# A Nyström attention and two mixture layers on one core: loads of 128 partitions, another grouping of heads, G split straight from its banks, x copies on GpSimd, both squares on ScalarE

## The chip, the core and the metric

The kernel runs on one core of one Trainium2 chip. The core has a matrix engine (PE; its weight loads are shown apart as PEld), VectorE (DVE), ScalarE (ACT), GpSimd (POOL) and SyncE (SP), which here issues nearly all DMAs. The metric is the device time of one execution in microseconds (us).

## The reference

Attention with 32 landmarks over 8 batches, 8 heads, 576 tokens and 64 columns a head; its output x (4608 × 512) goes through a layer with a squared relu, then through one of eight experts for each token.

```python
q_lm = q.reshape(B, H, m, S // m, D).mean(axis=3)     # k_lm alike, m = 32
A, Bm, C = sm(q, k_lm), sm(q_lm, k_lm), sm(q_lm, k)   # scaled softmax of a @ b.T
Z = Bm.T / (norm_1(Bm) * norm_inf(Bm) + 1e-06)
for _ in range(6):
    Z = 2 * Z - Z @ Bm @ Z
x = heads_side_by_side(A @ Z @ C @ v)
x = square(maximum(x @ w_in, 0)) @ w_out              # 512 -> 2048 -> 512
e_idx = argmax(x @ w_gate)                            # one expert for each token
out = gate_w * eom * (maximum(x @ w1[e_idx], 0) @ w2[e_idx])
```

## The kernel before

**Order of the products.** For each batch and head the kernel forms the 32 × 64 matrix wz = Z·C·v, then G = wz·w_in, and only then the product with A: hp = G·Aᵀ is the hidden layer itself. Each operand of a large product is split into two float32r parts, a rounded one and the rest, and three products of parts stand for one (`gb`, `ab`, `wo` hold such pairs).

**The main loop.** `gemm(b, c, f)` goes over 8 batches b, two halves c of 288 tokens and 16 blocks f of 128 hidden rows. For each f PE writes hp (six matmuls) into the pool `hps`, which has one PSUM bank, so the six of f+1 can't begin before ACT has read hp of f. ACT makes r = relu(hp) and gh, its square rounded to float32r; DVE makes g2 = r·r in full and gl = g2 − gh. Two f later (`pend`) `second` runs twelve matmuls of wo with gh and gl into four accumulator banks.

**The side work.** While `gemm` runs batch b, the attention unit of batch b+1 goes along in small steps (`point`, paced by RATES): `sums` of 18 rows for the landmarks (on POOL from batch 2 on), `flipped` (turns a group of four heads of q or k by 32 × 32 transposes on DVE, L480 and L484; two heads then lie on the wrong partitions, so two copies of 32 × 576 on ACT, L491, carry others over, and two transposes of 32 partitions, which overwrite what the copies read, follow them; the two groups of a k or q go together, so four copies come at one place, two places a batch), scores, softmax, `inverse`, `values`. `transposed` does the work of `flipped` on PE for the first two batches. Near the end of a batch `next_g` makes the four G of the next one: eight matmuls into a pair of banks (`two`), an ACT copy gs of each bank (L995), a few steps later an ACT cast gb and two POOL subtracts (`halves`) for the second part.

**The beginning.** `prologue` computes the first batch's unit with nothing to lie beside. Meanwhile `convert` fetches w_in and w_out, which lie in DRAM as 8-byte floats, in pieces of 128 × 512 (`raw`, 524 kB each, four buffers); ACT and POOL make floats of them (`m`, `r`, then `wf` or `w`). Four wf make one G of the first batch, and `first_g` makes two G before the main loop; each wf is also written to DRAM (`win`) for the later batches. Loads of q, k (four DMAs of 32 partitions for a group of four heads), v (three DMAs of 32 partitions), raws and the win writes stand in one queue, SP's.

**Order.** A scheduler sets each engine's order from priorities (URGENT for r, g2, gh, gl and all of the prologue); on each engine instructions then run strictly in that order. After the loop `experts` runs the expert layer, which the change does not touch.

Of the kernel before, what the change touches and what calls it, by code (L numbers as in the profile page):

```python
# [44 lines left out]
CONV = 0.45  # L45
CONV_FIRST = 2
# [24 lines left out]
def head_of(g, j):  # L71

    return j // 2, 2 * g + j % 2
# [18 lines left out]
class Kernel:  # L92
    def __init__(self, tc, ins, out):
# [6 lines left out]
        self.gt, self.at, self.made, self.g_done, self.last_gb, self.last_lo = {}, {}, {}, 0, None, None  # L100
        self.wf, self.wo, self.qk, self.vt, self.wts, self.wis = {}, {}, {}, {}, {}, {}


    def after(self, n, fn):

        self.later.append((self.now + n, fn))

# [115 lines left out]
    def convert_in(self):  # L223

        def job(i):
            n, kp = divmod(i, KD)

            def place():
# [6 lines left out]
                lambda w: self.nc.sync.dma_start(out=self.win_d[n][:, kp], in_=w),  # L235
# [22 lines left out]
    def run(self):  # L258
        tc = self.tc
        with ExitStack() as ctx:  # L260
# [31 lines left out]
            def swap():  # L292
                tmp.close()
                self.wi, self.gs = T("wi", 2), T("gs", 2)
                out_pools(T)
                self.loads = iter([(b, n) for b in range(1, B) for n in range(4)])
                for _ in range(2):
                    self.load_w()
# [109 lines left out]
    def load_next(self, pool=None):  # L408
# [6 lines left out]
        src = (self.k if nm == "k" else self.q)[b, 4 * hg:4 * hg + 4].rearrange("(a g) (l s) d -> g a l (s d)", g=2, s=SEG)  # L415
        for g in range(2):
            for a in range(2):
                p = 64 * g + LM * a
                self.nc.sync.dma_start(out=t[p:p + LM].rearrange("p s d -> p (s d)"), in_=src[g, a])

    def load_v(self, b, g, pool=None):
        if b < B:
            t = self.vt[b, g] = (pool or self.ld).tile([PT, 4, R6 * D], F32, tag="v", name="v", bufs=1)
            src = self.v[b].rearrange("(j g) (l i r) d -> g i l j (r d)", g=2, i=3, r=R6)[g]
            for i in range(3):
                self.nc.sync.dma_start(out=t[LM * i:LM * i + LM], in_=src[i])

    def sums(self, u, nm, hg):
# [4 lines left out]
        if not u["pe"]:  # L433
# [20 lines left out]
    def transposed(self, u, nm, hg, i):  # L454
# [14 lines left out]
        if i == 2 and not (u["b"] == 0 and nm == "q" and hg == 1):  # L469
            self.load_next()  # L470

    def flipped(self, u, nm, hg):
# [17 lines left out]
        for h in (0, 2):  # L490
            self.nc.scalar.copy(out=x[LM * h + LM:LM * h + 2 * LM, 0], in_=x[LM * h:LM * h + LM, 1])  # L491
# [73 lines left out]
    def scores_c(self, u, i):  # L565
# [5 lines left out]
        for g, c, sc in self.products(u, "k", "ql", i):  # L571
            to, src = u["ec"][:, g], sc
            if u["pe"]:
                to = to.rearrange("p (r c i l) -> p c i r l", c=2, i=3, l=LM)[:, c]
                src = src.rearrange("p (i r l) -> p i r l", i=3, l=LM)
            else:
                to = to[:, c * HC:(c + 1) * HC]
# [85 lines left out]
    def values(self, u, hg):  # L663
# [3 lines left out]
        with self.run_of():  # L667
            for r in reversed(range(R6)):
                for h in reversed(range(4)):
# [3 lines left out]
                        rhs=self.vt[b, hg][:, h, r * D:(r + 1) * D],  # L673
# [8 lines left out]
        elif hg == 1:  # L682
            self.load_v(b + 1, 0)

    def inverse(self, u, i):
# [13 lines left out]
        if i == 6:  # L699
            u["wz"] = sm.tile([128, 2, D], F32, tag="wz", name="wz")  # L700
            nc.vector.tensor_tensor(out=u["wz"], in0=was[:, :, LM:], in1=pp[:, :, LM:], op=ALU.add)
# [15 lines left out]
        nc.scalar.copy(out=eu[:, :, 0:LM], in_=pp[:, :, 0:LM])  # L717
        nc.vector.tensor_tensor(out=eu[:, :, LM:], in0=was[:, :, LM:], in1=pp[:, :, LM:], op=ALU.add)

# [56 lines left out]
    def last_values(self, u):  # L776
# [3 lines left out]
        u["wz"] = self.sm.tile([128, 2, D], F32, tag="wz", name="wz")  # L780
        self.nc.vector.tensor_copy(out=u["wz"], in_=w)
# [127 lines left out]
    def prologue(self, right):  # L909
# [15 lines left out]
        while True:  # L925
# [5 lines left out]
            due += CONV  # L931
# [6 lines left out]
    def first_g(self):  # L938

        self.banks = [self.acc]  # L940
        with self.tc.high_priority(URGENT):
# [3 lines left out]
            self.drain()  # L945
        self.banks = [self.aux]

    def chunk(self, b, n, rows):
# [6 lines left out]
        with self.run_of():  # L955
            for g in range(2):
                for j in range(4):
                    p = slice(64 * g, 64 * g + 64)
                    self.matmul(
                        banks[g][32 * j:32 * j + 32], lhsT=self.wts[b][p, 32 * j:32 * j + 32], rhs=rows(j)[p],  # L960
# [5 lines left out]
    def first_g_of(self, n):  # L966
# [5 lines left out]
        t = self.gt[0, n]  # L972
        for g in range(2):
            gb = nc.scalar.copy(out=t[:, 0, g], in_=banks[g])
            lo = nc.vector.tensor_tensor(out=t[:, 1, g], in0=banks[g], in1=t[:, 0, g].bitcast(F32), op=ALU.subtract)
            if n < G_FIRST:
                self.last_gb, self.last_lo = gb, lo
# [8 lines left out]
    def next_g(self, b, n):  # L986
# [5 lines left out]
        t = self.gt[b, n]  # L992
        for g in range(2):
            raw = self.gs.tile([128, 512], F32, tag="gs", name="gs")
            self.nc.scalar.copy(out=raw, in_=banks[g])  # L995
# [550 lines left out]
```

## Time and profile before

| what | value |
|---|---|
| three runs | 1317.33, 1319.91, 1320.98 us (median 1319.91) |
| profiled execution | 1318.15 us, span 1316.3 us |
| PE busy | 1223.3 us, 93% of the span |
| DVE, ACT, POOL busy | 692.7, 590.3, 480.2 us |
| mean granted clock of PE | 0.977 |

The span runs from the first to the last instruction on the engines, and the profiled execution's own time stands 1.9 us above it. The first G begins at 59.57 us; the loop's first batch ends shortly before 200 us, batches 1 to 5 go to about 717 us, batches 6 and 7 to 893 us, and the experts take the rest. A row of a view gives start and length of an instruction, its engine, line and operation, output and input tiles, shape, and in brackets how long the engine had waited and for what.

### The profile page before, as it was taken

The numbers are of one execution on the slowest core, as the hardware profiler recorded it, in microseconds if no ns is written. First come the engines' busy times: TensorE is split into PE (matmuls) and PEld (weight loads), VectorE is DVE, ScalarE is ACT, GpSimd is POOL, SyncE is SP. The second block draws the span as 40 slices with busy tenths as digits, with TensorE's granted clock in tenths as the row PEclk, the third lists the DMA queues.
The fourth block names the chain that finished last, engine by engine and source line by source line (L and its number), as shares of the span: only waits on it lengthen the run. The fifth ranks groups of instructions, "written<-read, shape, count | busy, mean of one in ns | idle before, by whom it ended". The sixth has DMA issues, their size and how long they took to land.

```text
span 1316.3 us, 25740 instructions
## 1 busy us (share of the span) xinstructions
PE 1223.3 (93%) x9834; PEld 1086.7 (83%) x9834; DVE 692.7 (53%) x1641; ACT 590.3 (45%) x1316; POOL 480.2 (36%) x627
## 2 busy tenths in 40 slices
PE   3578899899999999999999999999999999999996
PEld 2367887878888988888888989998888988888885
DVE  5487765865765864864864745453333323233231
ACT  4556464464464464464355354343333424334231
POOL 3776724424432415415313221033333424324220
PEclk9689999999999999999999999999999999999998
DMA  9965324233133124123114220025344445353331
GB/s 255 335 187 153 118 95 119 62 101 120 55 101 119 54 72 146 40 88 132 37 51 151 67 83 19 20 56 147 103 120 142 125 122 147 96 157 88 110 92 38
DMA packets 90205, 142.29 MB, mean 108 GB/s; under 512 B 8222, under 2 KB 63550, under 8 KB 86494
## 3 DMA queue, kind: packets, MB, share of 16 engines
q1 hardware_dynamic: 89646, 139.98, 35.4%
q8 instruction: 79, 1.29, 0.4%
q0 software_dynamic: 288, 0.43, 0.1%
q14 instruction: 48, 0.39, 0.1%
q10 hardware_dynamic: 144, 0.20, 0.0%
HBM read 117.47 MB, written 23.11 MB: 107 GB/s over the span
## 4 chain that ended last, share of the span: by engine, by line
PE 76%; DVE 7%; DMA 5%; ACT 4%; POOL 3%; issue 2%; SPq 1%; DVEq 0%; POOLq 0%; ACTq 0%
PE hp L393 28%; PE acc L393 25%; PE y L393 16%; PE two L389 2%; DMA t<-in_q_dram 2%; PE bank L389 2%; DVE x L480 2%; DMA raw<-in_moe_w_in_dram 2%; PE bank L401 1%; DVE gl L1059 1%; POOL st L436 1%; ACT x L491 1%; DVE x L484 1%; POOL gb L221 1%; DMA v<-in_v_dram 1%
## 5 line engine op out<-in xcount | busy, mean ns | idle before, releaser
L393 PE MATMUL acc<-gh,wo 128*128 128x288 f32 x2048 | 450.9, 299 | 7.0 <-DVE wo L215 6.5
L393 PEld LDWEIGHTS acc<-gh,wo 128*128 128x128 f32 x2048 | 342.0, 190 | 19.2 <-DVE wo L215 8.1
L393 PE MATMUL acc<-gl,wo 128*128 128x288 f32 x1024 | 294.1, 301 | 2.4 <-DVE gl L1059 2.4
L393 PE MATMUL hp<-ab,gb 128*128 128x288 f32 x1536 | 262.9, 307 | 31.4 <-ACT r L1056 29.9
L393 PEld LDWEIGHTS hp<-ab,gb 128*128 128x128 f32 x1536 | 217.8, 191 | 59.1 <-ACT r L1056 39.8
L1057 DVE TENSOR_TENSOR g<-r 128x288 f32<-128x288 f32 x256 | 140.8, 551 | 194.2 <-ACT r L1056 192.3
L393 PE MATMUL y<-s,h 128*128 128x512 f32 (+1 forms) x896 | 223.0, 396 | 0.8 <-ACT h L1291 0.5
L393 PEld LDWEIGHTS hp<-xs,s 128*128 128x128 f32 x1536 | 212.3, 188 | 7.4 <-DVE ls L1502 0.3
L393 PE MATMUL hp<-xs,s 128*128 128x288 f32 x1536 | 217.4, 295 | 0.2 <-DVE ls L1502 0.2
L393 PEld LDWEIGHTS acc<-gl,wo 128*128 128x128 f32 x1024 | 195.4, 191 | 13.5 <-DVE gl L1059 5.8
L1056 ACT ACTIVATE r<-hp 128x288 f32<-128x288 f32 x256 | 105.3, 411 | 207.2 <-PE hp L393 190.4
L393 PEld LDWEIGHTS y<-s,h 128*128 128x128 f32 (+1 forms) x896 | 160.7, 184 | 37.8 <-ACT h L1291 0.7
L221 POOL TENSOR_TENSOR s<-r,s 128x256 fp32r<-128x256 f32 x128 | 102.1, 819 | 235.5 <-ACT s L209 235.5
L1059 DVE TENSOR_TENSOR gl<-g,gh 128x288 fp32r<-128x288 f32 x256 | 144.3, 564 | 37.0 <-ACT gh L1058 19.9
L1294 DVE SCALAR_TENSOR_TENSOR h<-hp,h 128x64 fp32r<-128x64 f32 (+2 forms) x192 | 62.4, 354 | 166.3 <-ACT h L1291 165.9
L221 POOL TENSOR_TENSOR gb<-gs,gb 128x256 fp32r<-128x256 f32 x112 | 90.4, 837 | 135.9 <-ACT gb L1000 135.9
L1291 ACT ACTIVATE h<-hp 128x288 fp32r<-128x288 f32 x128 | 52.5, 412 | 187.8 <-PE hp L393 172.3
L1058 ACT ACTIVATE gh<-r 128x288 fp32r<-128x288 f32 x256 | 114.1, 446 | 39.3 <-PE acc L393 26.2
L209 ACT CAST s<-r 128x512 fp32r<-128x512 f32 x128 | 77.6, 617 | 69.9 <-PE y L393 56.0
L215 DVE TENSOR_TENSOR s<-r,s 128x512 fp32r<-128x512 f32 x64 | 50.2, 784 | 101.6 <-ACT s L209 101.6
L436 POOL TENSOR_TENSOR st<-t 128x288 f32<-128x288 f32 x48 | 42.1, 897 | 96.7 <-DMA t<-in_q_dram 92.0
L221 POOL TENSOR_TENSOR aa<-aa,ma 128x288 f32<-128x288 f32 x60 | 44.2, 760 | 80.2 <-DVE ma L551 60.2
(201 smaller groups left out, 1128.1 us busy)
## 6 DMA issues: line engine op xcount, KB each, us to landing
r<-in_moe_w_dram SPq DMA_DIRECT2D x128, 256.0 KB
wi<-win SPq DMA_DIRECT2D x28, 1024.0 KB
t<-in_k_dram SPq DMA_DIRECT2D x64, 144.0 KB
t<-in_q_dram SPq DMA_DIRECT2D x64, 144.0 KB
v<-in_v_dram SPq DMA_DIRECT2D x48, 192.0 KB
x_d<-x SPq DMA_DIRECT2D x16, 576.0 KB
xr<-x_d SPq DMA_DIRECT2D x16, 576.0 KB
raw<-in_moe_w_in_dram SPq DMA_DIRECT2D x16, 511.8 KB
```

What stands on the lines that cost most here:

```text
L209: hi = self.nc.scalar.copy(out=t[:, 0], in_=raw)
L215: lo_eng.tensor_tensor(out=t[:, 1], in0=raw, in1=t[:, 0].bitcast(F32), op=ALU.subtract)
L221: self.nc.gpsimd.tensor_tensor(out=out[:, p], in0=in0[:, p], in1=in1[:, p], op=op)
L389: self.in_run(lambda: self.nc.tensor.matmul(out, **kw))
L393: mm = self.nc.tensor.matmul(out, **kw)
L436: add = lambda out, in0, in1: self.nc.gpsimd.tensor_tensor(out=out, in0=in0, in1=in1, op=ALU.add)
L1056: nc.scalar.activation(out=r, in_=hp[:, 0:HC], func=ACTF.Relu)
L1057: nc.vector.tensor_tensor(out=g2, in0=r, in1=r, op=ALU.mult)
L1058: nc.scalar.activation(out=gh, in_=r, func=ACTF.Square)
L1059: nc.vector.tensor_tensor(out=gl, in0=g2, in1=gh.bitcast(F32), op=ALU.subtract)
L1291: nc.scalar.activation(out=h[:, t0:t1], in_=hp[:, 0:HC], func=ACTF.Relu)
L1294: nc.vector.scalar_tensor_tensor(out=h[:, to + a:to + z], in0=hp[:, a - t0:z - t0], scalar=0.0, in1=h[:, a:z].bitcast(F32), op0=ALU.max, o ...
```

## The change

A group of four heads of q or k is now loaded by one DMA over 128 partitions, in the natural order of heads, and v by two DMAs of 96 partitions. Which head stands where follows: `head_of`, the operands of `chunk` and `values` and the layout of the scores change, and wz is put together with its halves crossed on every second group of 32 partitions (four DVE instructions in place of one). G of the later batches is split as that of the first was: ACT casts from the bank, DVE subtracts from the bank; gs and the POOL halves go. The four copies in `flipped` move from ACT to POOL, g2 from DVE to ACT, the copy eu in `inverse` from ACT to DVE, and the sums of one early q group from DVE to POOL. `hold` keeps win writes, the loads of the second batch's q, k and v back until the first G in program order, and the first eight wf are converted at a rate of 0.8 a step.

```diff
 def head_of(g, j):
 
-    return j // 2, 2 * g + j % 2
+    return j // 2, 3 - j % 2 if g else j % 2
...
+    def hold(self, fn):
+
+        if self.held is None:
+            fn()
+        else:
+            self.held.append(fn)
...
-                lambda w: self.nc.sync.dma_start(out=self.win_d[n][:, kp], in_=w),
+                lambda w: self.hold(lambda: self.nc.sync.dma_start(out=self.win_d[n][:, kp], in_=w)),
...
-        src = (self.k if nm == "k" else self.q)[b, 4 * hg:4 * hg + 4].rearrange("(a g) (l s) d -> g a l (s d)", g=2, s=SEG)
-        for g in range(2):
-            for a in range(2):
-                p = 64 * g + LM * a
-                self.nc.sync.dma_start(out=t[p:p + LM].rearrange("p s d -> p (s d)"), in_=src[g, a])
+        src = (self.k if nm == "k" else self.q)[b, 4 * hg:4 * hg + 4]
+        self.nc.sync.dma_start(
+            out=t.rearrange("p s d -> p (s d)"), in_=src.rearrange("h (l s) d -> (h l) (s d)", s=SEG)
+        )
...
-            src = self.v[b].rearrange("(j g) (l i r) d -> g i l j (r d)", g=2, i=3, r=R6)[g]
-            for i in range(3):
-                self.nc.sync.dma_start(out=t[LM * i:LM * i + LM], in_=src[i])
+            src = self.v[b].rearrange("(a g i) (p r) d -> a g p i (r d)", g=2, i=2, r=R6)
+            for a in range(2):
+                self.nc.sync.dma_start(out=t[:, 2 * a:2 * a + 2], in_=src[a, g])
...
-        if not u["pe"]:
+        if not u["pe"] or u["early"] and nm == "q" and hg == 1:
...
-            self.load_next()
+            self.hold(self.load_next)
...
         for h in (0, 2):
-            self.nc.scalar.copy(out=x[LM * h + LM:LM * h + 2 * LM, 0], in_=x[LM * h:LM * h + LM, 1])
+            self.nc.gpsimd.tensor_copy(out=x[LM * h + LM:LM * h + 2 * LM, 0], in_=x[LM * h:LM * h + LM, 1])
...
-            self.load_v(b + 1, 0)
+            self.hold(lambda: self.load_v(b + 1, 0))
...
+            for j in range(4):
+                p = slice(32 * j, 32 * j + 32)
+                nc.vector.tensor_tensor(
+                    out=self.crossed(wz, j), in0=was[p, :, LM:], in1=pp[p, :, LM:], op=ALU.add
+                )
...
-        nc.scalar.copy(out=eu[:, :, 0:LM], in_=pp[:, :, 0:LM])
+        nc.vector.tensor_copy(out=eu[:, :, 0:LM], in_=pp[:, :, 0:LM])
...
+    def crossed(self, wz, j):
+
+        t = wz[32 * j:32 * j + 32]
+        return t[:, ::-1] if j % 2 else t
...
-            due += CONV
+            due += CONV if len(self.wf) >= G_FIRST * KD else CONV_SOON
...
+        held, self.held = self.held, None
+        for fn in held:
+            fn()
         self.banks = [self.aux]
...
-        t = self.gt[b, n]
-        for g in range(2):
-            raw = self.gs.tile([128, 512], F32, tag="gs", name="gs")
-            self.nc.scalar.copy(out=raw, in_=banks[g])
-            self.after(2 + g, lambda g=g, raw=raw: self.split_g(t, g, raw))
-
-    def split_g(self, t, g, raw):
-
-        self.nc.scalar.copy(out=t[:, 0, g], in_=raw)
-        self.halves(t[:, 1, g], raw, t[:, 0, g].bitcast(F32), ALU.subtract)
+        self.split_g(self.gt[b, n], banks)
+
+    def split_g(self, t, banks):
+
+        nc = self.nc
+        for g in range(2):
+            gb = nc.scalar.copy(out=t[:, 0, g], in_=banks[g])
+            lo = nc.vector.tensor_tensor(out=t[:, 1, g], in0=banks[g], in1=t[:, 0, g].bitcast(F32), op=ALU.subtract)
+        return gb, lo
...
                     nc.scalar.activation(out=r, in_=hp[:, 0:HC], func=ACTF.Relu)
-                    nc.vector.tensor_tensor(out=g2, in0=r, in1=r, op=ALU.mult)
                     nc.scalar.activation(out=gh, in_=r, func=ACTF.Square)
+                    nc.scalar.activation(out=g2, in_=r, func=ACTF.Square)
                     nc.vector.tensor_tensor(out=gl, in0=g2, in1=gh.bitcast(F32), op=ALU.subtract)
```

**SP, from its first instruction on.** t is a group of q or k, raw a piece of w_in, win the copy of w_in in DRAM. Before:

```order
L419 DMA t<-in_k_dram 32x1152 x8
L419 DMA t<-in_q_dram 32x1152 x3
L419 DMA t<-in_k_dram 32x1152 x4
L419 DMA t<-in_q_dram 32x1152
L419 DMA t<-in_k_dram 32x1152 x4
L419 DMA t<-in_q_dram 32x1152 x4
L161 DMA raw<-in_moe_w_in_dram 128x2047 x3
L426 DMA v<-in_v_dram 32x4x384 x6
L161 DMA raw<-in_moe_w_in_dram 128x2047 x2
L235 DMA win_124<-wf 128x512
L161 DMA raw<-in_moe_w_in_dram 128x2047 x2
L235 DMA win_124<-wf 128x512 x2
```

And now:

```order
L425 DMA t<-in_k_dram 128x1152 x2
L425 DMA t<-in_q_dram 128x1152 x2
L170 DMA raw<-in_moe_w_in_dram 128x2047 x3
L434 DMA v<-in_v_dram 96x2x384 x4
L170 DMA raw<-in_moe_w_in_dram 128x2047
L425 DMA t<-in_k_dram 128x1152 x2
L170 DMA raw<-in_moe_w_in_dram 128x2047
L244 DMA win_112<-wf 128x512
L170 DMA raw<-in_moe_w_in_dram 128x2047 x2
L244 DMA win_112<-wf 128x512 x2
L170 DMA raw<-in_moe_w_in_dram 128x2047
L244 DMA win_112<-wf 128x512
```

A group of heads is one row's DMA instead of four, the first q stands behind two k instead of behind eight loads, and the k of the second batch (the third and fifth rows before, the pair behind the fourth raw now) has moved behind four raws.

**ACT, in batch 2's first half, beside the flip of a later batch's k.** r, gh and g are the relu and the squares, x the copies, aa an exponential, eu a copy of the inverse. Before:

```order
L1056 ACTIVATE r<-hp 128x288
L1058 ACTIVATE gh<-r 128x288
L491 COPY x<-x 32x576 x2
L1056 ACTIVATE r<-hp 128x288
L491 COPY x<-x 32x576 x2
L1058 ACTIVATE gh<-r 128x288
L1056 ACTIVATE r<-hp 128x288
L557 ACTIVATE aa<-aa 128x576
L717 COPY eu<-bank 128x2x32
L1058 ACTIVATE gh<-r 128x288
L557 ACTIVATE aa<-aa 128x576
L1056 ACTIVATE r<-hp 128x288
```

And now, at the same place:

```order
L1076 ACTIVATE r<-hp 128x288
L1077 ACTIVATE gh<-r 128x288
L1078 ACTIVATE g_4227<-r 128x288
L1076 ACTIVATE r<-hp 128x288
L1077 ACTIVATE gh<-r 128x288
L1078 ACTIVATE g_4262<-r 128x288
L565 ACTIVATE aa<-aa 128x576
L1076 ACTIVATE r<-hp 128x288
L1077 ACTIVATE gh<-r 128x288
L1078 ACTIVATE g_4301<-r 128x288
L565 ACTIVATE aa<-aa 128x576
L1076 ACTIVATE r<-hp 128x288
```

The four copies and eu are gone from between r and gh, and one more square, g, stands behind each gh.

**POOL, at the same flip.** gb is the split of G, ab and aa parts of the attention matrix, st and sums the landmark sums. Before:

```order
L436 TENSOR_TENSOR sums<-st 128x128
L221 TENSOR_TENSOR gb<-gs,gb 128x256 x4
L221 TENSOR_TENSOR ab<-at,ab 128x288 x2
L221 TENSOR_TENSOR aa<-aa,ma 128x288 x4
L436 TENSOR_TENSOR st<-t 128x288 x2
L436 TENSOR_TENSOR st<-st 128x256
L436 TENSOR_TENSOR st<-st 128x128
L221 TENSOR_TENSOR aa<-aa,ma 128x288 x2
```

And now:

```order
L444 TENSOR_TENSOR sums<-st 128x128
L499 COPY x<-x 32x576 x2
L230 TENSOR_TENSOR ab<-at,ab 128x288 x2
L499 COPY x<-x 32x576 x2
L230 TENSOR_TENSOR aa<-aa,ma 128x288 x4
L444 TENSOR_TENSOR st<-t 128x288 x2
L230 TENSOR_TENSOR aa<-aa,ma 128x288 x2
```

The four gb halves are gone; two of the four copies stand ahead of ab, two behind it.

## Rows read from the trace of the kernel before

**Rows 1.** Busy time in three stretches; the columns stand in the first row.

```profile
core 0: us, PE busy (x) PEld busy (x) DVE busy (x) ACT busy (x) POOL busy (x), PEclk, DMA share, GB/s
59.60:200.00 140.40, 122.44 (x1062) 102.69 (x1063) 106.10 (x207) 83.90 (x193) 84.16 (x114) 0.94 0.50 152
200.00:717.00 517.00, 487.21 (x4502) 434.65 (x4501) 334.86 (x814) 254.57 (x606) 189.42 (x262) 0.99 0.29 89
717.00:893.00 176.00, 175.54 (x1411) 166.21 (x1411) 93.86 (x233) 76.56 (x179) 39.11 (x49) 1.00 0.19 58
```

**Rows 2.** ACT, then PE, in order of time, up to the first G.

```profile
49.31 0.77 ACT L173 ACTIVATE m<-raw 128x512 f16<-128x512 bf16 x1 [1.99 <-DMA raw<-in_moe_w_in_dram]
...
59.57 1.11 PE L389 MATMUL bank<-wf,wt 64*32 64x512 f32 x8
```

**Rows 3.** Waits of PE, 200 to 717: total us, times, longest.

```profile
PE hp L393 <- ACT r L1056: 25.0, 23, 2.6
PE two L389 <- ACT gs L995: 1.6, 3, 0.9
```

**Rows 4.** PE in order of time: four of its 23 waits for r.

```profile
209.73 1.06 PE L393 MATMUL hp<-ab,gb 128*128 128x288 f32 x6 [2.58 <-ACT r L1056]
...
237.89 1.06 PE L393 MATMUL hp<-ab,gb 128*128 128x288 f32 x6 [1.09 <-ACT r L1056]
...
508.27 1.05 PE L393 MATMUL hp<-ab,gb 128*128 128x288 f32 x6 [1.48 <-ACT r L1056]
...
688.96 1.07 PE L393 MATMUL hp<-ab,gb 128*128 128x288 f32 x6 [1.40 <-ACT r L1056]
```

**Rows 5.** ACT in order of time, shortly ahead of the first two of these.

```profile
206.73 0.59 ACT L995 COPY gs<-two 128x512 f32<-128x512 f32 x1 [4.42 <-POOL gb L221]
...
235.71 1.37 ACT L491 COPY x<-x 32x576 f32<-32x576 f32 x2
```

**Rows 6.** Waits of ACT and of POOL, 200 to 717.

```profile
ACT gs L995 <- POOL gb L221: 24.2, 14, 4.4
...
POOL ab L221 <- ACT ab L209: 72.6, 7, 22.1
```

**Rows 7.** Groups, 200 to 717: count, busy us, mean ns, idle before.

```profile
L1057 DVE TENSOR_TENSOR g<-r 128x288 f32<-128x288 f32 x156 | 85.7, 550 | 117.1 <-ACT r L1056 115.9
...
L1058 ACT ACTIVATE gh<-r 128x288 fp32r<-128x288 f32 x157 | 69.9, 446 | 25.9 <-PE acc L393 15.0 <-DVE g L1057 3.9 <-DVE ma L559 3.7
...
L1059 DVE TENSOR_TENSOR gl<-g,gh 128x288 fp32r<-128x288 f32 x157 | 88.7, 565 | 23.2 <-ACT gh L1058 13.5 <-PE bank L401 0.9
...
L491 ACT COPY x<-x 32x576 f32<-32x576 f32 x40 | 26.8, 671 | 4.5 <-DVE x L480 3.3
...
L221 POOL TENSOR_TENSOR gb<-gs,gb 128x256 fp32r<-128x256 f32 x88 | 70.8, 833 | 84.0 <-ACT gb L1000 83.9
```

**Rows 8.** Groups of POOL, whole span, columns as in rows 7.

```profile
L452 POOL COPY sums<-sums 128x64 f32<-128x64 f32 x8 | 1.9, 240 | 22.6 <-DVE sums L447 22.6
...
L175 POOL CAST m<-raw 128x512 f16<-128x512 bf16 x24 | 19.0, 805 | 3.6 <-DMA raw<-in_moe_w_in_dram 3.6
...
L221 POOL TENSOR_TENSOR wf<-m,r 128x256 int32<-128x256 int32 x32 | 23.4, 760 | 8.0 <-ACT r L176 7.7
```

**Rows 9.** Waits of PE, 59.6 to 200.

```profile
PE acc L393 <- DVE wo L215: 6.5, 5, 3.0
PE hp L393 <- ACT r L1056: 5.0, 6, 1.5
```

**Rows 10.** DMA rate in stretches of the beginning, columns as in rows 1.

```profile
8.00:18.00 10.00, 3.32 (x12) 2.36 (x12) 4.33 (x4) 1.93 (x5) 0.51 (x3) 1.00 1.04 230
22.00:28.00 6.00, 3.19 (x51) 1.35 (x52) 2.29 (x8) 4.53 (x14) 4.82 (x7) 1.00 1.10 230
28.00:34.00 6.00, 4.86 (x52) 3.23 (x50) 4.37 (x20) 4.33 (x10) 3.11 (x5) 1.00 1.02 393
```

**Rows 11.** DVE in order of time, while POOL splits a G.

```profile
211.08 1.07 DVE L1059 TENSOR_TENSOR gl<-g,gh 128x288 fp32r<-128x288 f32 x1 [0.48 <-ACT gh L1058]
```

More of the change, by code (lines that the diff above doesn't have):

```diff
@@ L45 @@
 CONV = 0.45
+CONV_SOON = 0.8
 CONV_FIRST = 2
@@ L100, in __init__ @@
         self.gt, self.at, self.made, self.g_done, self.last_gb, self.last_lo = {}, {}, {}, 0, None, None
+        self.held = []
         self.wf, self.wo, self.qk, self.vt, self.wts, self.wis = {}, {}, {}, {}, {}, {}
@@ L293, in swap @@
                 tmp.close()
-                self.wi, self.gs = T("wi", 2), T("gs", 2)
+                self.wi = T("wi", 2)
                 out_pools(T)
@@ L573, in scores_c @@
             if u["pe"]:
-                to = to.rearrange("p (r c i l) -> p c i r l", c=2, i=3, l=LM)[:, c]
+                to = to.rearrange("p (r c l i) -> p c i r l", c=2, i=3, l=LM)[:, c]
                 src = src.rearrange("p (i r l) -> p i r l", i=3, l=LM)
             else:
-                to = to[:, c * HC:(c + 1) * HC]
+                to = to.rearrange("p (r l i) -> p r i l", i=3, l=LM)[:, 3 * c:3 * c + 3]
+                src = src.rearrange("p (r i l) -> p r i l", i=3, l=LM)
             nc.scalar.copy(out=to, in_=src)
@@ L672, in values @@
                         lhsT=u["et"][:, R6 * hg + r, 32 * h:32 * h + 32],
-                        rhs=self.vt[b, hg][:, h, r * D:(r + 1) * D],
+                        rhs=self.vt[b, hg][:, h ^ hg, r * D:(r + 1) * D],
                         start=(r == R6 - 1), stop=(r == 0),
@@ L699, in inverse @@
         if i == 6:
-            u["wz"] = sm.tile([128, 2, D], F32, tag="wz", name="wz")
-            nc.vector.tensor_tensor(out=u["wz"], in0=was[:, :, LM:], in1=pp[:, :, LM:], op=ALU.add)
+            wz = u["wz"] = sm.tile([128, 2, D], F32, tag="wz", name="wz")
+            for j in range(4):
[3 more added lines that the diff above has]
+                )
             return
@@ L779, in last_values @@
         self.blocks(w, u["ef"], u["w0"])
-        u["wz"] = self.sm.tile([128, 2, D], F32, tag="wz", name="wz")
-        self.nc.vector.tensor_copy(out=u["wz"], in_=w)
+        wz = u["wz"] = self.sm.tile([128, 2, D], F32, tag="wz", name="wz")
+        for j in range(4):
+            self.nc.vector.tensor_copy(out=self.crossed(wz, j), in_=w[32 * j:32 * j + 32])
     def diagonal(self, u, x):
@@ L957, in chunk @@
                 for j in range(4):
-                    p = slice(64 * g, 64 * g + 64)
+                    half = g ^ (j % 2)
+                    p = slice(64 * half, 64 * half + 64)
                     self.matmul(
-                        banks[g][32 * j:32 * j + 32], lhsT=self.wts[b][p, 32 * j:32 * j + 32], rhs=rows(j)[p],
+                        banks[g][32 * j:32 * j + 32], lhsT=self.wts[b][p, 32 * j:32 * j + 32],
+                        rhs=rows(2 * (j // 2) + g)[p],
                         start=True, stop=True,
@@ L971, in first_g_of @@
         banks = self.chunk(0, n, lambda j: self.wf[n * KD + j])
-        t = self.gt[0, n]
-        for g in range(2):
[L974 to L977, printed above, removed]
+        gb, lo = self.split_g(self.gt[0, n], banks)
+        if n < G_FIRST:
+            self.last_gb, self.last_lo = gb, lo
     def load_w(self):
```

## The prediction

> **What bounds the kernel now.** I read the busy time by stretches first, since one change rarely acts on the whole span. From 717 to 893 us PE is busy 175.54 of 176.00 us [rows 1], so nothing can be won there, and the experts behind it are not touched. From 200 to 717 us PE is busy 487.21 of 517.00, which leaves 29.8 us of idle time; from 59.6 to 200 it is 122.44 of 140.40, which leaves 18.0. Ahead of 59.6 PE has not begun its large products: the eight matmuls of the first G stand at 59.57, and on ACT a conversion at 49.31 still waited 1.99 us for a piece of w_in by DMA [rows 2]. So there are three places: the loads of the beginning, the first batch, and the five batches after it.
>
> In the five batches the chain of waits is short. PE waited 25.0 us in 23 waits for r, before the first product of a new hp, and 1.6 us for gs [rows 3]. Looked up in order of time, 21 of the 23 (20.9 us) fall at ten places where ACT makes the four x copies, two in each batch: the first is the 1.09 us at 237.89 and the last the 1.40 at 688.96; the other two, 2.58 at 209.73 and 1.48 at 508.27, 4.1 us together, are not at such a place [rows 4]. What ACT did just ahead shows why. At 235.71 it ran two x copies in a row, 1.37 us, while r and the squares stood behind them; at 206.73 a gs copy had waited 4.42 us for a gb subtract of POOL to free its buffer [rows 5], one of 14 such waits of 24.2 us in all [rows 6]. On average DVE is busy 334.86 and ACT 254.57 of 517 us [rows 1]; it is their order at a dozen places that costs.
>
> **The change part by part.**
>
> *Five batches, 200 to 717 us.* 157 f in 517 us are 3.3 us each. ACT loses the 40 copies of 671 ns, 26.8 us, and takes a square of 446 ns (the row of gh, which is the same operation on the same shape) for each f, 70 us [rows 7]. It also loses 40 gs copies of 0.59 us (five batches, four G, two banks), 24 us. Its busy time goes from 255 to about 275 of 517: no bound. DVE loses 85.7 us of g2 and takes 40 subtracts of 512 columns, each at most 1.0 us (565 ns of gl, for 288 columns, scaled). POOL loses 70.8 us of gb and takes 40 copies.
> At a place with copies ACT loses 4 × 0.671 = 2.7 us and gains the three squares that stand there among its twelve rows, 1.3 us. Net 1.35 us against a wait of 20.9 / 10 = 2.1 us: if the squares count in full, 13.5 us come back at the ten places; if they fit into ACT's idle time between two r, all 20.9. I take 16, nearer the lower end, because ACT is late exactly there.
> The waits for gs (1.6) and for r behind gs (4.1) lose their cause, since nothing on ACT waits for POOL's subtract any more; in its place the pair of banks comes free only after DVE's second subtract. Nothing gained to 5.7; I take 5, since the next G follows two or three f later.
> The square delays the next r elsewhere only where ACT is late for another reason. The 20 G are such places, with two casts; at most 20 × 0.446 = 8.9 us, at least 0; I take 3, because r is not ready before hp is, and PE's waits for r lie only at the places named.
> Sum: −16 − 5 + 3 = −18, bounds −26.6 and −4.6. The copies of eu, 64 columns, which ACT loses and DVE takes, and the three more small adds for wz are counted at nothing: they lie beside PE's matmuls and help ACT where they hurt DVE; if DVE were the late one, they would cost about what the copy of 64 columns on POOL shows, 240 ns [rows 8], five or six times a batch.
>
> *First batch, 59.6 to 200 us.* Here DVE is the late engine: PE waited 6.5 us for the split of wo on DVE and 5.0 for r [rows 9]. Sixteen g2 of the first half leave DVE, 8.8 us of 550 ns, and 7.1 us of squares come to ACT, which was busy 83.90 of 140.40 [rows 1]. I take −3; bounds −9 (most of both waits) and +7 (all squares late).
>
> *The beginning.* SP's order is what decides, so I counted it up to the eleventh raw, the one that ACT waited for. Before and now the same bytes stand ahead of it: 28 loads of 32 × 1152 floats or their equal (4.13 MB), 1.18 MB of v, eleven raws, five win writes. So the hold itself moves nothing on this queue, and what is left is the rate. With loads of 32 partitions the queues moved 230 GB/s from 8 to 18 us, with those of v 230 from 22 to 28, and with raws of 128 partitions 393 from 28 to 34, all with the DMA engines fully busy [rows 10]. At 393 the q and k take 10.5 us instead of 18.0: −7.4. v on 96 partitions lies between 230 and 393, so 0 to −2.1; I take −1. ACT now converts 15 pieces instead of 14 ahead of the first wt; a piece takes one pass r and every second time a pass m on ACT, 0.77 us a pass [rows 2], so +1.2. Together −7, bounds −9.5 and 0.
> The Trainium skill, "SBUF — State Buffer", section "Door 1: The DMA port swizzle", says that a transfer of 32 partitions reaches half of the sixteen ports into SBUF; the trace agrees, 230 against 393 GB/s. By its table 96 partitions reach all ports, but half of these carry twice the rows: an estimate of 12/16 of 393, 295 GB/s, by which v would save 1.1 us and the sum would stay.
>
> *All.* −18 − 3 − 7 = −28. The profiled execution took 1318.15 us, so 1290 us for one like it; the median of the runs is 1.76 above it, so **1292 us**. By the bounds of the parts the same case goes from 1275 to 1322.
>
> **Rivals.**
>
> *The loads don't bring the first G forward (1299 us).* Between the wait at 49.31 and the first G at 59.57 lie 10 us without one for DMA [rows 2]. If raws come 7 us sooner, the conversion must keep up: POOL gives each raw two halves of 760 ns and every second one a cast of 805 ns [rows 8], 1.9 us, and gets eight adds of an early q besides (at most 6 us by the same 760); ACT and the scores share the rest. Then part or all of the 7 us is lost. For it: the halves of wf waited 7.7 us for ACT's r [rows 8], so ACT holds the conversion up too; against it: the row at 49.31 waits for DMA, behind ten pieces. 1290 + 7 + 1.8 = 1299.
>
> *The squares are paid for (1307 us).* ACT carries the chain hp, r, gh, and an r that is late by one square holds PE. If it is late in 34 of the 157 f, seven a batch around G and softmax, that is 34 × 0.446 = 15 us of the 18 lost again: 1290 + 15 + 1.8 = 1307. For it: ACT was late at the ten places; against it: a mean idle time of half of ACT.
>
> *Slower (1336 us): the copies wait on POOL.* Of the twelve places six now have two copies ahead of ab on POOL and two behind it, as the order shows. POOL's ab waited 72.6 us in 7 waits for ACT, 10.4 each [rows 6]; the second pair stands behind that. The transposes of 32 partitions on DVE wait for the copies, and the gl of four following f stand among them. A copy of 32 × 576 is not in the trace on POOL. Its bounds are 240 ns (64 columns) and 805 (a cast of 512 columns) [rows 8]; along the line through both 576 columns cost 0.9 us. So the last copy comes 10.4 + 4 × 0.9 = 14 us late, gl has two f of slack, 6.6 us, and 7.4 us are lost at each of six places, +44. It outweighs the gain from 28 / 6 = 4.7 us a place, copies about 11 us late. Against it: ab's two parts were waited for since POOL had nothing else ready; the scheduler has put the copies there with ab's cast near in ACT's order, and all of ab's waits need not fall at flips.
> While POOL subtracted a G, a gl of DVE took 1.07 us [rows 11] against a mean of 565 ns [rows 7]: the two engines hold each other up. The Trainium skill, "SBUF — State Buffer", section "Who interferes with whom", says that a DVE instruction with two inputs in SBUF and a GpSimd instruction that reads SBUF exclude each other for a whole instruction; the row agrees in direction. By that rule each copy could start up to 0.57 us later, four of them 2.3, and this rival would be reached sooner by that; in return 157 g2 with two inputs leave DVE.
>
> **How the numbers follow.** The sum as worked out 0.60, the loads in vain 0.20, the squares paid for 0.11, the copies late 0.06, something else 0.03. The forecast is the first case's 1292 us. For 8 in 10 the range goes from 1276, a little above that case's lower bound, to 1314, which takes in the first two rivals and leaves out the third: 0.06 of it, 0.03 of the rest and some 0.08 of the tails lie outside. A difference of 0.3%, 4 us, is about what a measurement of this kernel can tell from no change. Faster than 1316: nearly all of the first three cases, 0.89; between 1316 and 1324: their tails, 0.04; above: the third rival and part of the rest, 0.07.
>
> **What would show it.** The DMA rate up to 20 us near 393 instead of 230, and the first G at about 52 us; if the rate is there and the G still at 59, the first rival holds. PE's waits for r from 200 to 717 at under 10 us instead of 25.0, none after an x copy, and none for gs; if they stand at other places behind a square, the second. POOL's x copies at about 0.9 us, and DVE's transposes of 32 partitions waiting for them: if more than 5 us at a place, with PE waiting for gl, the third. Stretches after batch 6 and the experts as long as before. The prediction is wrong above all if the order of the engines, which is fixed beforehand from estimated durations, puts an instruction ahead of r or gl that comes late on the chip: no row of the kernel before can show that.

## The result, and the profile after

The changed kernel takes **1259.53 us** (median of four runs, 1259.2 to 1260.13), against 1320.45 us for the kernel before on the same chip: a ratio of 0.9543, 95% interval 0.9527 to 0.9560. 61 us were gained where 28 were forecast, and the time lies below the range. Three single runs further on, one of a_x (1373.1 us), one of u_gs4 (2344.5) and one of the kernel before (1968.1), stood far above the others of their kernel, and the medians are without them.

To see where they went I read from ACT's rows in order of time when r was made for the 32nd and for the 192nd f: these mark the ends of the first batch and of batch 5, in either kernel.

| us | before | after | change | forecast |
|---|---|---|---|---|
| first G begins | 59.57 | 50.71 | −8.9 | −7 |
| first G to 32nd r | 125.3 | 119.2 | −6.1 | −3 |
| 32nd to 192nd r (batches 1 to 5) | 528.7 | 486.6 | −42.1 | −18 |
| 192nd r to the end of the span | 602.8 | 601.0 | −1.8 | 0 |

So the miss lies in batches 1 to 5. The first three rows below, of the changed kernel, answer to [rows 1], with its columns; the fourth is its batches 1 to 5, 169.91 to 656.49 us:

```profile
59.60:200.00 140.40, 129.83 (x1186) 113.31 (x1187) 89.44 (x186) 89.55 (x219) 79.89 (x112) 0.97 0.43 149
200.00:717.00 517.00, 515.86 (x4816) 467.81 (x4816) 305.05 (x828) 278.24 (x706) 145.89 (x219) 1.00 0.28 93
717.00:893.00 176.00, 175.55 (x1259) 163.13 (x1259) 56.78 (x150) 86.06 (x200) 39.45 (x38) 1.00 0.23 69
...
169.91:656.49 486.58, 485.44 (x4596) 436.57 (x4595) 294.09 (x775) 266.10 (x676) 148.25 (x224) 1.00 0.29 99
```

And the same five batches of the kernel before, with a piece of them around one flip:

```profile
184.88:713.54 528.66, 496.79 (x4586) 441.88 (x4585) 347.51 (x852) 263.55 (x627) 187.70 (x260) 0.99 0.29 89
...
430.90:433.90 3.00, 1.26 (x8) 0.83 (x6) 2.88 (x5) 2.98 (x7) 1.92 (x4) 1.00 0.00 0
433.90:437.10 3.20, 3.04 (x12) 3.04 (x13) 3.11 (x7) 0.11 (x1) 0.00 (x0) 0.51 0.75 199
```

PE's idle time fell from 31.9 us (528.66 − 496.79) to 1.1. That is 30.7 of the 42.1. The other 11.4 are in PE's *busy* time, 496.8 against 485.4 for the same products. The last two rows show most of it: PE had been busy for 1.26 of 3.00 us, and then its granted clock was 0.51, which is 1.2 instead of 2.4 GHz. Read in pieces of 3 us, the five batches of before have four such places (430, 530, 580 and 640 us) with 13.7 us at the low clock; those of after have none. At half speed 13.7 us do the work of 6.8, so 6.8 us is what the clock took if PE had work throughout. The 4.6 us left over are in stalls too short to show as idle: they are argued, not shown.

PE's waits from 200 to 717 us, where [rows 3] had 25.0 us for r and 1.6 for gs, are one row:

```profile
PE acc L402 <- DVE gl L1079: 1.1, 3, 0.6
```

The groups that answer to [rows 7] and to the price of an x copy (200 to 717 us; g is the square that is new on ACT):

```profile
L1079 DVE TENSOR_TENSOR gl<-g,gh 128x288 fp32r<-128x288 f32 x172 | 87.7, 511 | 114.5 <-ACT g L1078 113.2
...
L1078 ACT ACTIVATE g<-r 128x288 f32<-128x288 f32 x172 | 74.1, 431 | 0.0
L1020 DVE TENSOR_TENSOR gb<-two,gb 128x512 fp32r<-128x512 f32 x42 | 29.0, 692 | 28.7 <-ACT gb L1019 28.5
L499 POOL COPY x<-x 32x576 f32<-32x576 f32 x40 | 27.6, 689 | 179.5 <-DVE x L488 102.7 <-DVE x L492 75.0
```

An x copy takes 689 ns on POOL, below the 0.9 us worked out, and the copies wait for DVE's transposes, not for ab. The rates that answer to [rows 10], and the first G:

```profile
4.00:10.00 6.00, 4.05 (x20) 3.65 (x20) 5.65 (x8) 3.08 (x7) 0.47 (x2) 1.00 1.02 368
10.00:16.00 6.00, 0.48 (x1) 0.18 (x1) 0.99 (x1) 2.35 (x5) 4.79 (x9) 0.60 1.05 341
...
22.00:28.00 6.00, 4.44 (x35) 3.85 (x36) 4.54 (x23) 5.54 (x16) 1.46 (x3) 0.50 1.04 403
```

```profile
50.71 3.67 PE L398 MATMUL bank<-wf,wt 64*32 64x512 f32 x32 [0.89 <-ACT wt L816]
```

### The profile page after: what moved, and what is told of

It is laid out like the page before. It is cut to its first block, busy times and chain, and to the rows that moved or that the text cites. A ratio compares the mean times of both kernels' runs of the same rounds, so it can differ in the third digit from the quotient of the medians.

```text
span 1257.5 us, 25149 instructions
## 1 busy us (share of the span) xinstructions
PE 1206.7 (96%) x9834; PEld 1078.6 (86%) x9834; DVE 591.3 (47%) x1498; ACT 615.2 (49%) x1433; POOL 421.3 (34%) x568
## 4 chain that ended last, share of the span: by engine, by line
PE 90%; DVE 3%; DMA 3%; ACT 2%; POOL 1%; issue 1%; SPq 0%; POOLq 0%; ACTq 0%; DVEq 0%
PE acc L402 32%; PE hp L402 32%; PE y L402 17%; PE two L398 4%; PE bank L398 2%; PE bank L410 1%; DMA raw<-in_moe_w_in_dram 1%; PE pl L398 1%; DMA v<-in_v_dram 1%; PE pt L1168 1%; DVE x L488 1%; DMA t<-in_q_dram 1%; DVE gl L1079 1%; ACT r L185 0%; DVE ma L559 0%
## 5 line engine op out<-in xcount | busy, mean ns | idle before, releaser
L402 PE MATMUL acc<-gl,wo 128*128 128x288 f32 x1024 | 288.9, 298 | 1.1 <-DVE gl L1079 1.1
L402 PE MATMUL hp<-ab,gb 128*128 128x288 f32 x1536 | 255.7, 301 | 1.6 <-ACT r L1076 1.5
L1079 DVE TENSOR_TENSOR gl<-g,gh 128x288 fp32r<-128x288 f32 x256 | 131.4, 514 | 198.8 <-ACT g L1078 192.6
L1078 ACT ACTIVATE g<-r 128x288 f32<-128x288 f32 x256 | 110.6, 432 | 5.3 <-DVE gl L1079 5.0
L499 POOL COPY x<-x 32x576 f32<-32x576 f32 x48 | 33.9, 706 | 195.7 <-DVE x L488 102.7
L230 POOL TENSOR_TENSOR xs<-xr,xs 128x576 fp32r<-128x576 f32 x32 | 45.9, 1459 | 64.0 <-ACT xs L218 48.0
```

The costliest lines, as they stand in the source:

```text
L230: self.nc.gpsimd.tensor_tensor(out=out[:, p], in0=in0[:, p], in1=in1[:, p], op=op)
L402: mm = self.nc.tensor.matmul(out, **kw)
L1078: nc.scalar.activation(out=g2, in_=r, func=ACTF.Square)
L1079: nc.vector.tensor_tensor(out=gl, in0=g2, in1=gh.bitcast(F32), op=ALU.subtract)
```

## The experiments

Each kernel below ran beside the kernel before, whose medians went from 1318.0 to 1320.5 us; so a difference of some 2 us says little. Differences in the text are of medians; 1259.5 is the changed kernel. Times of batches are those of the profiled execution. "Undone" means the changed kernel with one part as before; "alone" the kernel before with one part of the change. The scheduler lays out the order of all engines anew for each kernel, so a part undone moves other instructions too.

**The parts undone.**

u_x, the copies on ACT:

```diff
-            self.nc.gpsimd.tensor_copy(out=x[LM * h + LM:LM * h + 2 * LM, 0], in_=x[LM * h:LM * h + LM, 1])
+            self.nc.scalar.copy(out=x[LM * h + LM:LM * h + 2 * LM, 0], in_=x[LM * h:LM * h + LM, 1])
```

> The changed kernel with the x copies of the flips back on ACT, all else as changed. Theory A (ACT's copies ahead of r made the stalls at the flips): the 21 us of waits for r at ten places come back, and the granted clock falls again after some of them, some 7 us: about 1285 us. Theory B (the stalls came from DVE, where g2 stood behind the transposes and r waited for its buffer): the copies cost ACT's idle time, at most 5 us: 1260 to 1265, PE's waits for r under 6 us. Theory C (either alone is enough to stall, the two together made it worse): 1270 to 1278.

u_g2, the square on DVE:

```diff
+                    nc.vector.tensor_tensor(out=g2, in0=r, in1=r, op=ALU.mult)
                     nc.scalar.activation(out=gh, in_=r, func=ACTF.Square)
-                    nc.scalar.activation(out=g2, in_=r, func=ACTF.Square)
```

> The changed kernel with the full square g2 back on DVE, all else as changed. Theory A (ACT's copies): the square on ACT was only a cost, so 1256 to 1260, and PE's waits for r stay under 3 us. Theory B (g2 behind the transposes on DVE, r waiting for its buffer): the stalls at the flips come back, with the clock: about 1285. Theory C (both): 1268 to 1278. All of them: in the first batch DVE is late again, some 3 us.

u_gs, the split over gs and POOL (`split_late` is split_g of before):

```diff
-        self.split_g(self.gt[b, n], banks)
+            raw = self.gs.tile([128, 512], F32, tag="gs", name="gs")
+            self.nc.scalar.copy(out=raw, in_=banks[g])
+            self.after(2 + g, lambda g=g, raw=raw: self.split_late(t, g, raw))
```

> The changed kernel with G of the later batches split as before (copy gs and cast gb on ACT, subtracts on POOL), all else as changed. By the prediction's step the waits behind gs come back: 5 us, 1264 to 1266. If POOL, which has the x copies now, delays gs further or holds the copies back behind 80 halves, more: 1270 or above. If gs was no cause of its own: 1259 to 1261.

u_load, the loads in pieces of 32 partitions:

```diff
+        for h in range(4):
             self.nc.sync.dma_start(
-            out=t.rearrange("p s d -> p (s d)"), in_=src.rearrange("h (l s) d -> (h l) (s d)", s=SEG)
+                out=t[LM * h:LM * h + LM].rearrange("p s d -> p (s d)"),
+                in_=src[h].rearrange("(l s) d -> l (s d)", s=SEG),
```

> The changed kernel with each load of q and k cut into four of 32 partitions and each of v into three of 32, the same bytes to the same places. By the prediction's step the beginning loses its 230 to 393 GB/s: the first G 7 to 9 us later than 50.7, 1266 to 1269 us in all, and nothing changes after it. If the first batch's gain was made by other parts (the adds on POOL, the eu copies, the order of conversions), the first G moves by less than 3 us: about 1261.

| undone | median | against 1259.5 | batches 1 to 5 | ratio to before, 95% |
|---|---|---|---|---|
| u_x | 1268.83 | +9.3 | 497.3 (+10.7) | 0.9622, 0.959 to 0.9654 |
| u_g2 | 1275.79 | +16.3 | 495.8 (+9.2) | 0.9673, 0.9641 to 0.9704 |
| u_gs | 1278.68 | +19.2 | 503.9 (+17.3) | 0.9690, 0.9658 to 0.9723 |
| u_load | 1280.60 | +21.1 | 486.8 (+0.2) | 0.9717, 0.9683 to 0.9752 |

Neither theory A nor B holds for the square and the copies; theory C, between them, comes nearest. Each of three parts is worth 9 to 17 us in batches 1 to 5, 37 of the 42 together, and the loads act only ahead of them. For the loads 1266 to 1269 was expected and nothing behind the first G; yet 12 of their 21 us lie between it and the 32nd r.

**The parts alone.** a_x, a_g2 and a_gs make the first three edits the other way round in the kernel before; a_g2gs makes the second and the third.

> The kernel before with only the x copies moved from ACT to POOL. Additive theory (each part removes its own waits; undoing it cost 9.3 us): 1308 to 1311. Theory of common stalls (at a flip ACT's copies and DVE's g2 each are enough to hold r, so one alone gives little): 1313 to 1318, waits of PE for r still above 15 us. By the prediction's step (16 of 20.9 us come from the copies): 1300 to 1304.

> The kernel before with only the full square moved from DVE to ACT. Additive theory (undoing it cost 16.3 us): 1301 to 1304. Common stalls: 1310 to 1318. By the prediction's step the square on ACT is a cost of 3 us in the five batches against 3 us gained in the first: no change, about 1318, or worse beside the copies that are still on ACT.

> The kernel before with only G of the later batches cast and subtracted straight from its banks, gs and POOL's halves gone. Additive theory (undoing it cost 19.2 us): 1298 to 1301. By the prediction's step: 5 us, 1313. A loss, 1320 or more, if the subtracts of 512 columns on DVE, which still has every g2, hold r's buffers.

> The kernel before with two parts alone: the full square on ACT and G split straight from its banks; x copies stay on ACT. Additive theory (13.6 and 13.4 us for each alone): 1291. If the two remove the same waits: 1298 to 1304. If they help each other, since with both neither r's buffers nor ACT wait for another engine: 1282 to 1288.

Measured: a_x 1321.8 (ratio 1.0026, 0.9998 to 1.0055: no gain), a_g2 1304.61 (0.9890, 0.9863 to 0.9918), a_gs 1304.83 (0.9904, 0.9874 to 0.9934), a_g2gs 1282.0 (0.9708, 0.9681 to 0.9736). Square and split together save 37 us, where the two alone, 13.6 and 13.4, make 27: they help each other. With the kernels above, batches 1 to 5 are on record for all eight combinations of the three parts:

| moved | kernel | batches 1 to 5, us |
|---|---|---|
| none | before | 528.7 |
| copies | a_x | 532.0 |
| square | a_g2 | 518.6 |
| split | a_gs | 514.1 |
| copies, square | u_gs | 503.9 |
| copies, split | u_g2 | 495.8 |
| square, split | a_g2gs; u_x | 498.8; 497.3 |
| all three | after | 486.6 |

So the copies on POOL are worth nothing only where they are the only change: beside the square they give 14.7 us, though POOL still splits G there, beside the split 18.3, beside both 10.7 to 12.2. The u kernels have the loads and the small parts as well. Taken out of the changed kernel these move the five batches by less than 1 us (u_load above, u_eu and u_begin below). Whether the copy eu, ahead of which ACT waits 39.2 us for DVE in these batches of the kernel before, is worth more beside fewer of the other parts is not tested; some of the 14.7 and the 18.3 may be its.

Batches 1 to 5 of a_x, then its waits of PE and of ACT in them:

```profile
189.90:722.00 532.10, 504.44 (x4586) 448.99 (x4585) 349.07 (x852) 236.16 (x583) 218.20 (x304) 0.97 0.29 89
```

```profile
PE hp L393 <- ACT r L1056: 13.2, 9, 5.4
PE acc L393 <- DVE gl L1059: 6.3, 9, 0.8
...
ACT gs L995 <- POOL gb L221: 24.6, 10, 7.0
```

PE's waits for r are halved against before (26.4 us in the same batches there), yet nothing is gained. They are fewer and longer, up to 5.4 us, since gs waits up to 7.0 us for a POOL that has copies to make as well. Waits for others, gl above all, came up, so that PE's whole idle time fell only from 31.9 us to 27.7 (532.10 − 504.44). And, read in the same pieces of 3 us, the clock fell at nine places instead of four, 34 us at the low level instead of 13.7: at half speed 20 us more there are 10 us of work. PE's busy time, 504.4 us instead of 496.8, takes back more than the waits gave. The runs of a_x agree: the fastest, 1313.1 us, had a mean granted clock of 0.976, the slowest, 1330.7, one of 0.965. The profile is of one of 1326.4.

**Work or buffers?** u_gs4 is u_gs with four gs buffers; u_g2r4 is u_g2, and b_r4 the kernel before, with four buffers for r and the square; b_buf is the kernel before with three each of r, square and gs; after_r4 is the changed kernel with four for r and the square.

```diff
-                self.wi, self.gs = T("wi", 2), T("gs", 2)
+                self.wi, self.gs = T("wi", 2), T("gs", 4)
...
-                r = self.g3.tile([128, HC], F32, tag="r", name="r")
+                r = self.g3.tile([128, HC], F32, tag="r", name="r", bufs=4)
```

> The changed kernel with the split of G over gs and POOL as in the run that undid it, but four gs buffers instead of two, so that a gs copy no longer waits for POOL's subtract of the G before. If the wait for that buffer is what the old split cost: 1261 to 1266, PE's waits for r under 4 us. If the cost is the second pass on ACT (0.6 us for each of 56 banks) or POOL's load beside the copies: 1273 to 1279, as with two buffers.

> The changed kernel with the full square back on DVE, as in the run that undid it (1275.8), and four buffers for r and the square in place of two. If r waited for its buffer until DVE had squared: most of the 16 us comes back, 1260 to 1266, and ACT's waits of r for DVE's square (10.5 us there) vanish. If DVE's time itself is the limit (square, difference and transposes in one queue): 1272 to 1277.

> The kernel before with four buffers for r and the square instead of two, nothing moved. If r's buffer is the path by which the square on DVE cost 13.6 us: 1304 to 1310. If the work on DVE is: 1315 to 1320, no change.

> The kernel before with three buffers each for r, the square and gs instead of two, nothing moved. If buffers are the path for both parts, it comes near the run that moved both: 1282 to 1295. If the work on the engines decides: 1312 to 1320.

> The changed kernel with four buffers for r and the square instead of two. PE waits 1.5 us for r in it, so by the waits there is nothing to win: 1258 to 1261. If some waits too short to be seen between PE's instructions come from r's buffers: 1252 to 1257.

Measured: u_gs4 1268.8, u_g2r4 1274.17, b_r4 1317.47 (ratio 0.9985, 0.9968 to 1.0002), b_buf 1306.41 (0.9908, 0.9872 to 0.9943), after_r4 1258.19 (0.9545, 0.9512 to 0.9579: no change against the changed kernel). r's buffers are not the path: four of them win back 1.6 of the square's 16 us and nothing in the kernel before. gs's are: in batches 1 to 5 u_gs takes 503.9 us and u_gs4 491.8. ACT's longest waits of gs there, in u_gs and then in u_gs4, where POOL is no longer what it waits for:

```profile
ACT gs L1016 <- POOL gb L230: 16.4, 9, 3.9
```

```profile
ACT gs L1016 <- PE two L398: 12.1, 14, 1.5
```

So of the 17.3 us of the split 12.1 were a buffer that POOL freed late, and 5.2 remain for the second pass on ACT and POOL's share (by the medians of the whole it is 9.9 of 19.2). With r's buffers out, DVE's time is left for the square: batches 1 to 5 of u_g2 (its busy times, then a wait of PE and one of its weight loads)

```profile
177.40:673.20 495.80, 489.81 (x4598) 438.08 (x4597) 365.59 (x936) 216.74 (x517) 152.69 (x224) 1.00 0.29 96
```

```profile
PE hp L402 <- ACT r L1076: 3.2, 6, 0.6
...
PEld acc L402 <- DVE g L1077: 6.6, 11, 0.8
```

show no long wait, but DVE busy for 366 of 496 us instead of 294 of 487. Weight loads of the second products wait, 0.6 us at a time, for a DVE that is making a square; but in the changed kernel the same loads wait nearly as much for ACT:

```profile
PEld acc L402 <- ACT gh L1077: 5.0, 6, 0.8
```

So for batches 1 to 5 DVE's time is argued, not shown. In the first batch a wait shows it: PE's waits for the split of wo on DVE, in u_g2 and then in the changed kernel:

```profile
PE acc L402 <- DVE wo L224: 7.9, 5, 3.8
```

```profile
PE acc L402 <- DVE wo L224: 2.6, 2, 1.7
```

**The small parts and the beginning.** u_eu puts the copy of eu back on ACT. u_begin takes out the hold, the pace of 0.8 and the early q's sums on POOL. u_load0 and u_load1 cut only batch 0's, or only the later batches', loads, by the edit of u_load behind `if b == 0:` or `if b > 0:`. h_real makes the held DMAs follow the eleventh piece of w_in:

```diff
+        self.bar = self.raws[10]
         for fn in held:
             fn()
...
+    def behind_raw(self, dma):
+        if self.bar is not None:
+            self.follow(dma, self.bar)
```

> The changed kernel with only the copies of eu back on ACT, 35 of 64 columns. By the prediction (counted at nothing): 1259 to 1261. If ACT, waiting in order for DVE's dg ahead of each copy, holds r back: 5 us or more, 1264 to 1270, with PE's waits for r at the inverses.

> The changed kernel without the hold, with the old pace of the first conversions and with the sums of the early q back on DVE; loads stay as changed. By the prediction (the hold moves nothing on SP, the sums and the pace count little): 1258 to 1261. If batch 1's q and v ahead of the eighth piece of w_in delay the first G: their 1.2 MB at 393 GB/s, 3 us, 1262 to 1264. If the first batch falls into the longer course that the cut loads showed: 1268 or above.

> The changed kernel with only batch 0's loads of q, k and v cut into pieces of 32 partitions. If the 21 us that all loads in pieces cost lie in the beginning alone: 1279 to 1281. If the beginning is worth the 7.8 us by which the first G came later then, and the rest is the loads of later batches beside the weights: 1266 to 1269.

> The changed kernel with only the loads of batches 1 to 7 cut into pieces of 32 partitions. If these take DMA time from the pieces of w_in and w_out in the first batch: the first G within 2 us of 50.7, the first batch 8 to 13 us longer, 1268 to 1273, and batches 1 to 5 as long as changed. If all of the loss lay in the beginning: 1260.

> The changed kernel with the hold made real on SP: the writes of win and the loads of batch 1's k, q and v are ordered behind the eleventh piece of w_in. Theory that pieces of w_in set the first G, through ACT's conversions ahead of the exponentials: 3.1 MB less ahead of the pieces, 7.8 us at 393 GB/s, of which half or more arrives: 1252 to 1256. Theory that the chain of batch 0's attention is the limit by now: first G within 2 us of 50.7, and batch 1's k late for the transposes behind it: 1258 to 1264.

| kernel | median | ratio to before, 95% | first G | 32nd r |
|---|---|---|---|---|
| before | 1320.45 | 1 | 59.57 | 184.88 |
| after | 1259.53 | 0.9543, 0.9527 to 0.9560 | 50.71 | 169.91 |
| u_load | 1280.60 | 0.9717, 0.9683 to 0.9752 | 58.49 | 189.91 |
| u_load0 | 1273.41 | 0.9663, 0.9633 to 0.9692 | 51.15 | 182.80 |
| u_load1 | 1263.53 | 0.9575, 0.9552 to 0.9599 | 56.52 | 174.48 |
| h_real | 1262.15 | 0.9568, 0.9548 to 0.9588 | 53.87 | 172.66 |
| u_begin | 1266.20 | 0.9606, 0.9589 to 0.9623 | 41.28 | 175.30 |
| u_eu | 1258.88 | 0.9545, 0.9530 to 0.9561 | 51.81 | 170.6 |

eu's copy was rightly counted at nothing in the changed kernel. The rest upsets the step on the beginning. u_begin starts its first G 9.4 us *earlier* than the changed kernel and ends its first batch 5.4 us *later*; u_load0 starts it at the same time and ends 12.9 later; u_load1, with the loads of batch 0 wide and its first G expected within 2 us of the changed kernel's, starts 5.8 later. From here on the first G says little: what counts is when the first batch is through, with all of w_in and w_out converted. From the first r to the 32nd in the changed kernel, then the same 871 matmuls in u_load0:

```profile
61.43:169.91 108.48, 99.34 (x871) 87.50 (x870) 67.62 (x136) 69.26 (x170) 68.44 (x93) 0.96 0.40 138
```

```profile
61.50:182.80 121.30, 105.43 (x871) 90.88 (x872) 71.23 (x138) 72.09 (x172) 71.66 (x99) 0.92 0.40 138
```

Of the 12.8 us half, 6.1, is PE's busy time at a lower mean clock (0.92 against 0.96), half its idle time. One wait of 3.4 us, of PE for a subtract `gb` on DVE that frees the pair of banks, is new; the rest is spread. Which part of the order of DMAs and conversions makes these waits stays open: each kernel has its own order, and none had the slow loads in the order of the changed kernel. h_real, which keeps 3.1 MB back behind eleven pieces of w_in, has a median 2.6 us higher, with intervals of the ratios that overlap: the first G comes 3.2 us later, not sooner. No kernel here is faster than the changed one by more than a measurement can tell.

## Why the prediction was wrong

*The direction and the chain of reasoning on the places were right*: idle time of PE from 200 to 717 us, waits for r and gs, loads at 230 GB/s. All of these went. Less than half of the gain was forecast, and four steps failed: the sign of the square, the size of the split, one size for the copies whatever the rest, and a term for the clock that was not there. They overlap, since the parts act on one another, and do not add up to the miss.

*"The square delays the next r elsewhere only where ACT is late for another reason ... I take 3."* The sign was wrong. Undoing it alone costs 16 us, 9 of them in batches 1 to 5 and 7 in the first batch. I priced the square on ACT, where it came, and priced DVE, where it left, as an engine with time to spare; but in the kernel before DVE's queue is what r's products and wo's split stand in (the waits for wo above show it in the first batch; in batches 1 to 5 it is argued). Between +3 and −9 in batches 1 to 5 lie 12 us.

*"Nothing gained to 5.7; I take 5"* for the split of G. It measured 17.3 in batches 1 to 5, outside my bounds. ACT's 24.2 us of waiting for POOL stood in [rows 6], but I let only the two waits count that had a wait of PE of their own, 4.1 us, and 1.6 for the pair of banks. ACT works in order: a gs that waits 4 us makes each r, gh and x copy behind it late. So more waits fell than the 4.1 us: a_gs still has every copy on ACT, and its waits for r in these batches are 15.6 us instead of 26.4, all 15 of them shortly behind x copies. What made the split dear was gs's buffer: four of them won back 12.1 us (u_gs4).

*"I take 16"* for the copies. They gave 10.7 when all else was changed, 18.3 beside the split and nothing alone. The 20.9 us at the ten places had more causes than one, and the sum gave them to one; that 16 lies between these values is no proof of the step.

*A term was missing.* At four places PE's waits cost more than their length, since the granted clock fell behind them: up to 6.8 us of 42. The row of [rows 1] with 0.99 held it; I read it as full speed. a_x shows the other side of it: half of the waits for r gone and no time gained, in part because the clock fell more often.

*The beginning.* The rates came nearly as forecast (368 GB/s from 4 to 10 us, where q and k load, against 230 in [rows 10]), and the first G came 8.9 us earlier. But that the −7 came so near was in part luck: with batch 0's loads in pieces again the rate from 4 to 10 us is 204 GB/s and the first G stands at 51.15, 0.4 us later (u_load0), and it is the later batches' loads in pieces that put it at 56.52 (u_load1). That the loads are worth 7 us was mis-sized: undoing them costs 21, 7.8 ahead of the first G and the rest in the first batch. "The hold itself moves nothing on this queue" was true against the kernel before only; with wide loads and no hold, batch 1's q stands ahead of the eighth piece of w_in and its v ahead of the ninth, where the changed kernel has them behind the ninth and the eleventh, and the three parts of the beginning together are worth 6.7 us (u_begin). The forecast for the first batch, −3 by DVE's 16 squares, was too small for the same reason as in the other batches (−6.1; undoing the square costs 7 there).

*The rivals.* The loads in vain: no. The squares paid for: no, the opposite. The copies late on POOL: not in the changed kernel, where the copies wait for DVE's transposes and no row shows DVE or gl waiting for a copy; but its mechanism is what a_x shows, with gs in the place of ab. That DVE and POOL hold each other up, the traces show more clearly than [rows 11]: from 200 to 640 us of the kernel before a gl took 456 ns on the mean with no POOL instruction beside it, 765 beside a subtract of G on POOL and 670 beside another POOL instruction, 1068 at most; in the changed kernel, where POOL splits no G, 455 and 618. The rule of the Trainium skill, "SBUF — State Buffer", section "Who interferes with whom", that a DVE instruction with two inputs in SBUF contends with a GpSimd instruction that reads SBUF, agrees with this.

## What to carry to other kernels

When an engine with an in-order queue (here ACT) feeds the one that bounds the time, count every wait in its queue as a possible cause of the waits behind, not only those that show as a wait of the bounding engine beside them; what one part of a change removes can hide behind another part's wait, so parts that are worth nothing alone (a_x) can be worth 9 us and more beside others. Price a moved instruction at the engine that it leaves as well as at the one that it joins. And before trusting "the first product starts 9 us earlier", look at what must be finished with it: in u_begin an earlier start of the first batch was followed by a later end.

## What the runs showed of the hardware

- The clock can cost on top of the wait, and it can take little: after one wait of 1.10 us and another of 0.80 PE's granted clock went from 1.00 to 0.51. Waits of PE in the kernel before, around 432 us, the second row of six matmuls taking 1.81 us instead of 1.07:

```profile
432.19 1.07 PE L393 MATMUL hp<-ab,gb 128*128 128x288 f32 x6 [1.10 <-ACT r L1056]
434.06 1.81 PE L393 MATMUL hp<-ab,gb 128*128 128x288 f32 x6 [0.80 <-ACT r L1056]
```

It does not do so each time: behind waits of 1.09 us at 237.89 and 0.84 at 239.80 the clock stayed at 1.00.

- A copy of 32 × 576 takes 689 ns on POOL and 671 on ACT; a subtract of 512 columns from a PSUM bank 692 ns on DVE; a gl, of 288 columns with both inputs in SBUF, takes 455 with POOL idle, which scales to 0.81 us.
- A buffer more can be worth as much as work moved: a third buffer for gs, r and the square, with nothing moved, took 12 us off the kernel before (b_buf), nearly as much as either part alone; four buffers for r and the square without gs's (b_r4) took off nothing that can be told.
